# Everything behind the opening of a one-core attention and gated-MLP kernel as one written list of 1072 steps, with w_down of six token tiles by seven block products per pair

## The chip, the cores and the metric

The kernel runs on one core of one Trainium2 chip. The metric is the device time of an execution in microseconds (us), from launch to the last store; lower is better. The time before is the median of three runs.

## What is computed

A layer norm of 2048 tokens of width 512 feeds two branches in parallel, and both are added to the input:

```python
xn = layernorm(x)                                   # 2048 x 512
# A: linear attention, 32 heads of 16
q, k, v = split(xn @ wqkv)
phi_q = concat(softmax(q @ w_phi), softmax(-q @ w_phi))     # per head, 32 features
phi_k = the same of k
kv, z = phi_k^T v, sum of phi_k                     # per head, over the tokens
A = (phi_q kv / (phi_q z + 1e-6)) @ wo
# B: gated MLP without a nonlinearity
B = ((xn @ w_gate) * (xn @ w_up)) @ w_down          # 512 -> 1792 -> 512
out = x + A + B
```

Everything comes and goes in bf16.

## The kernel before

Tokens are worked in 16 tiles of 128; four tiles are a group of 512. x, all weights and the hidden values stay on the chip. Each engine runs its instructions in the order in which the program emits them (`manual_schedule`), so the order of the code is the order of the work, and a wait of one instruction holds all behind it on its engine.

- The opening (lines 550 to 602) loads, normalises and transposes the first four tiles, with v of these and half of two hidden units. TensorE's first instruction behind it is the second half of unit 0 (`unit(0, f, 2 * P, TT)`, line 627). All loads are issued at the top (lines 92 to 110) on SyncE's queue, in the order x, w_v, first columns of w_gate and w_up, the transposed w_k, then w_gate and w_up columns for units 2 to 3, 4 to 8 (around x tiles 4 to 7), 9 to 13, x from 8, w_down and w_o. The transposed load of w_q is issued at line 659, behind all transposes of x tiles 4 to 7.
- A unit (T, f) is 128 of the 1792 hidden columns for one group of 512 tokens: four matmuls for the gate, four for up, a copy of the gate out of PSUM (`gate_copy`, ScalarE), a multiplication on VectorE (`hidden`). Groups 0 and 1 are made so, 28 units.
- `fold` multiplies w_phi into the weights of k and q; `features` makes the softmax features: two exponentials on ScalarE, sums and reciprocals on VectorE, a multiplication on GpSimd. phi of q and the attention output `o_tok` are transposed by DMA (SyncE).
- Groups 2 and 3 of the gate and up products use Strassen's scheme in Winograd's form over pairs of blocks: `pair_block` has seven products p1 to p7, whose parts are kept (`keep`), joined (`join`) and multiplied. Its operands are differences of weights (`weight_sums`, line 445: GpSimd or VectorE, from bf16 to f16) and of tokens (`token_sums`); weights are scaled by powers of two first (`weight_norm`, line 420, `weight_scales`, `weight_up`).
- `fin_parts` (line 387) multiplies hidden values by w_down and attention output by w_o into one PSUM bank of 512 columns per tile: 14 + 4 matmuls. The store adds x on VectorE (line 398) and sends 128 KB. The last tile is cut into 384 and 128 columns.
- Order: hand-written loops with `ffn(1)` and `chore()` between projections, then `run_blocks` with fillers, then tiles 9 to 15 one after the other. Buffers rotate: of six PSUM banks of `ps_s` each new tile takes the next in turn.

Of the kernel before, what the change touches and what calls it, by code (L numbers as in the profile page):

```python
# [8 lines left out]
BF16 = mybir.dt.bfloat16  # L9
# [9 lines left out]
def _bcast_ap(ap_in: bass.AP, new_ap):  # L19
    return bass.AP(tensor=ap_in.tensor, offset=ap_in.offset, ap=new_ap)  # L20


@with_exitstack
def kernel(
# [40 lines left out]
    consts = ctx.enter_context(tc.tile_pool(name="consts", bufs=1))  # L65
    wpool = ctx.enter_context(tc.tile_pool(name="wpool", bufs=1))
# [7 lines left out]
    wgu = wpool.tile([P, 2, DC, F], BF16)  # L74
# [60 lines left out]
    xnT = xpool.tile([P, DC, HALF], BF16)  # L135
# [11 lines left out]
    for i in range(NV):  # L147
        vt = vpool.tile([P, 8, 4, E1], BF16, name=f"vt{i}", tag="vt")
        nc.vector.memset(vt[:, :, :, DH:E1], 1.0)
        vts.append(vt)  # L150
# [9 lines left out]
    def bank(name, dt=F32, n=TT):  # L160
        return ps_s.tile([P, n], dt, name=name, tag="s")
# [26 lines left out]
    def subtract(n, *means):  # L188
        xns[n] = xnpool.tile([P, D], BF16, name="xn", tag="x")
        nc.vector.tensor_scalar(out=xns[n][:], in0=xall[:, n, :], scalar1=means[0],  # L190
                                scalar2=means[1] if len(means) > 1 else None, op0=ALU.subtract,
                                **(dict(op1=ALU.subtract) if len(means) > 1 else {}))
# [9 lines left out]
    def centre_by_halves(n):  # L202
        h = D // 2
        part = consts.tile([P, 2], F32)
        junk = xnpool.tile([P, 2, h], BF16, name="junk", tag="x")
# [5 lines left out]

    chores = []

    def chore(k=1):
        for _ in range(min(k, len(chores))):
            chores.pop(0)()

    def ln_block(lo):
        mv = mv_tile()
        nb = lnpool.tile([P, GT], F32, name="nb", bufs=GT)  # L220
        rstd = []

        def scales():
            r = lnpool.tile([P, GT], F32, name="rstd", bufs=GT)
            ln_rstd(mv, GT, r[:])
            nm = lnpool.tile([P, GT], F32, name="nm")
            nc.gpsimd.tensor_scalar(out=nm[:], in0=mv[:, :, 0], scalar1=-1.0, scalar2=None, op0=ALU.mult)
            nc.gpsimd.tensor_tensor(out=nb[:], in0=nm[:], in1=r[:], op=ALU.mult)
            rstd.append(r)

        def apply(i):
            late = lo + i >= QT
            xn = xnpool.tile([P, D], F16 if late else BF16, name="xn", tag="x")
            if late:
                nc.gpsimd.tensor_scalar(out=xn[:], in0=xall[:, lo + i, :], scalar1=rstd[0][:, i:i + 1],
                                        scalar2=nb[:, i:i + 1], op0=ALU.mult, op1=ALU.add)
            else:
                nc.scalar.activation(out=xn[:], in_=xall[:, lo + i, :], func=AF.Identity,
                                     scale=rstd[0][:, i:i + 1], bias=nb[:, i:i + 1])
            nc.sync.dma_start(out=xt(lo + i), in_=xn[:], transpose=True)  # L240

        for i in range(GT):
            chores.append(lambda i=i: ln_stats(lo + i, mv[:, i, :]))
        chores.append(scales)
        for i in range(GT):
            chores.append(lambda i=i: apply(i))
# [18 lines left out]
    def fold(qk, dst, j0):  # L265
        R = P // 2
        banks = [bank("pq").rearrange("p (j c x) -> p j c x", j=2, c=DC) for r in range(2)]
        for j in range(2):
            for c in range(DC):
                for r in range(2):  # L270
                    rows = slice(r * R, (r + 1) * R)
                    nc.tensor.matmul(banks[r][:, j, c, :], lhsT=wT2[rows, qk, c, (j0 + j) * P:(j0 + j + 1) * P],  # L272
                                     rhs=bd[rows, c, 4 * r:4 * r + 4, :].rearrange("p a b -> p (a b)"),
                                     start=True, stop=True)
        dv = dst[:, j0:j0 + 2, :].rearrange("p j (c r x) -> p r j c x", c=DC, r=2)
        nc.scalar.copy(out=dv[:, 0], in_=banks[0])
        nc.vector.tensor_copy(out=dv[:, 1], in_=banks[1])

    def fold_both(qk, dst):
        for j0 in (0, 2):  # L280
            fold(qk, dst, j0)
# [6 lines left out]
    def features(n, w, name, pf=None):  # L288
        if pf is None:
            pf = bank(name)  # L290
            proj(pf, n, w)
        e = epool.tile([P, NG, 2, 4 * DH], F32, name="e")
        pfv = pf.rearrange("p (g c) -> p g c", g=NG)
        nc.scalar.activation(out=e[:, :, 0, :], in_=pfv, func=AF.Exp,  # L294
                             scale=rst[:, n:n + 1] if n < GT else 1.0)
        nc.scalar.activation(out=e[:, :, 1, :], in_=pfv, func=AF.Exp,  # L296
                             scale=nrst[:, n:n + 1] if n < GT else -1.0)
        ev = e[:].rearrange("p g s (h f) -> p (g s h) f", f=DH)
        sums = epool.tile([P, 2 * H], F32, name="sums")
        nc.vector.tensor_reduce(out=sums[:], in_=ev, axis=AX.X, op=ALU.add)  # L300
        rs = epool.tile([P, 2 * H, 1], F32, name="rs")
        nc.vector.reciprocal(out=rs[:].rearrange("p a b -> p (a b)"), in_=sums[:])  # L302
        phi = epool.tile([P, NG, P], BF16, name=f"phi{name}", tag="phi", bufs=4)
        nc.gpsimd.tensor_tensor(out=phi[:].rearrange("p g (x f) -> p (g x) f", f=DH), in0=ev,  # L304
                                in1=rs[:].to_broadcast((P, 2 * H, DH)), op=ALU.mult)
        return phi

    sends = []

    def qproj(n, held=False, new_bank=bank):  # L310
        q_begin(n, new_bank)
        q_end(held)

    q_open = []

    def q_begin(n, new_bank):
        pf = new_bank("q")
        proj(pf, n, W1q, lower)
        q_open.append((n, pf))

    def q_end(held=False):
        q_rest()
        q_features(held)

    def q_rest():
        n, pf = q_open[0]
        proj(pf, n, W1q, upper)

    def q_features(held=False):
        n, pf = q_open.pop()  # L330
        phiq = features(n, W1q, "q", pf)

        def send():
            phiqTs[n] = qtpool.tile([P, NG, P], BF16, name="phiqT")
            nc.sync.dma_start(out=phiqTs[n][:], in_=phiq[:].rearrange("p g c -> p (g c)"), transpose=True)

        sends.append(send)
        if not held:
            qsend()

    def qsend():
        sends.pop(0)()

    hTs = {}
    units = [(T, f) for T in range(NGRP // 2) for f in range(FC)]

# [7 lines left out]
    def gate_copy(ps, n):  # L354
        g_sb = gpool.tile([P, TT], BF16, name="g_sb")
        nc.scalar.copy(out=g_sb[:, 0:n], in_=ps)  # L356
        return g_sb

    def hidden(T, f, ps, g_sb, lo, hi):
        if T not in hTs:  # L360
            hTs[T] = hpool.tile([P, FC, TT], BF16, name="hT", tag="h")
        nc.vector.tensor_tensor(out=hTs[T][:, f, lo:hi], in0=ps, in1=g_sb[:, 0:hi - lo], op=ALU.mult)  # L362

    def unit(T, f, lo=0, hi=TT):
        pg = half(wg, "g", T, f, lo, hi)
        pu = half(wu, "u", T, f, lo, hi)
        hidden(T, f, pu, gate_copy(pg, hi - lo), lo, hi)

    def ffn(k):
        for _ in range(k):  # L370
            if units:
                unit(*units.pop(0))

    def fin_parts(n, new_bank, lo=0, hi=D):
        T, t4 = n // GT, n % GT
        w = hi - lo
        held = []

        rows = [(hTs[T][:, f, t4 * P:(t4 + 1) * P], wd[:, f, lo:lo + w]) for f in range(FC)]
        rows += [(oTs[n][:, c, :], wo[:, c, lo:lo + w]) for c in range(DC)]  # L380
        if n == 2 * GT:
            rows = [row for f, row in enumerate(rows) if f % FH != FH - 1 or f >= FC] + [rows[FH - 1], rows[FC - 1]]

        def mm(i):
            if i == 0:
                held.append(new_bank("fin")[:, 0:w])
            nc.tensor.matmul(held[0], lhsT=rows[i][0], rhs=rows[i][1], start=(i == 0), stop=(i == len(rows) - 1))  # L387
            if i == len(rows) - 1:
                store(held[0])

        def store(ps):
            o_sb = opool.tile([P, w], BF16, name=f"o_sb{w}", bufs=3 if w == D else 1)
            xres = xall[:, n, lo:lo + w]
# [9 lines left out]
    def fin(n, cuts=(0, D)):  # L403
        for lo, hi in zip(cuts, cuts[1:]):
            for part in fin_parts(n, bank, lo, hi):
                part()
# [427 lines left out]
```

## Time and profile before

| | |
|---|---|
| median of three runs | 216.29 us (216.26 to 216.33) |
| the profiled execution | 215.67 us |
| its span, first to last instruction | 213.9 us |
| TensorE busy (1280 matmuls) | 210.1 us |
| VectorE / ScalarE / GpSimd busy | 163.2 / 125.0 / 129.2 us |
| granted TensorE clock | 1.00 throughout |

The profile is of one execution. PE is TensorE, PEld its weight loads, DVE VectorE, ACT ScalarE, POOL GpSimd, SP SyncE, on whose queue all DMAs are issued. L387 is line 387 of the kernel. A matmul of the page has a modelled end, so its cost is read from the distance between starts, or from the chain.

### The profile page before, as it was taken

Reading aid. Unit: us, or ns where it says so; the run is one execution under the profiler, and the core shown is the slowest. Engines: PE = TensorE matmul, PEld = TensorE weight load, DVE = VectorE, ACT = ScalarE, POOL = GpSimd, SP = SyncE. Lnnn points to the kernel's source line nnn. Section 1 sums busy time; section 2 is a strip of 40 time slices with the busy share of each in tenths; the row PEclk is TensorE's granted clock in tenths of the full one; section 3 lists DMA queues with packets and bytes.
Section 4 is the critical chain, followed back from the end, with each engine's and each line's share of the span. In section 5 each row is a group of like instructions: output and inputs, shape, how many; then the busy total and the mean of one; then the engine's idle time right before and its main releaser. Section 6 shows DMA issues by size and latency. Waiting matters only on the chain.

```text
span 213.9 us, 3610 instructions
## 1 busy us (share of the span) xinstructions
PE 210.1 (98%) x1280; PEld 101.7 (48%) x1280; DVE 163.2 (76%) x279; ACT 125.0 (58%) x219; POOL 129.2 (60%) x112
## 2 busy tenths in 40 slices
PE   8999999999999999999999999999999999999994
PEld 3664445444444444554444444444444444444543
DVE  5757979869867788887777897988969689776341
ACT  4635578998896999442666686868746352220000
POOL 3600557597895788859899497979788620333000
PEclk9999999999999999999999999999999999999999
DMA  5999995613022023234444202021120201333511
GB/s 152 266 281 385 374 287 87 91 26 75 0 51 52 0 49 81 66 40 112 100 101 100 49 0 52 0 74 25 48 49 3 74 26 34 91 98 98 126 49 49
DMA packets 47249, 19.91 MB, mean 93 GB/s; under 512 B 37504, under 2 KB 46976, under 8 KB 47104
## 3 DMA queue, kind: packets, MB, share of 16 engines
q1 hardware_dynamic: 47232, 19.69, 36.6%
q8 instruction: 10, 0.16, 0.3%
q14 instruction: 7, 0.06, 0.1%
HBM read 8.67 MB, written 2.10 MB: 50 GB/s over the span
## 4 chain that ended last, share of the span: by engine, by line
PE 98%; ACT 1%; DVE 0%; issue 0%
PE fin L387 29%; PE g L350 11%; PE u L350 11%; PE sa L487 11%; PE pv L285 7%; PE q L285 6%; PE k L285 6%; PE sc L487 6%; PE sb L487 3%; PE kv L622 2%; PE ab L686 2%; PE warm L554 2%; PE pq L272 1%; PE tp L253 1%; ACT k L493 0%; ACT xnT L256 0%
## 5 line engine op out<-in xcount | busy, mean ns | idle before, releaser
L387 PE MATMUL fin<-wd,hT 128*128 128x512 bf16 (+2 forms) x238 | 54.1, 366 | 0.0
L304 POOL TENSOR_TENSOR phiq<-e,rs 128x1024 bf16<-128x1024 f32 x16 | 30.9, 1934 | 25.6 <-DVE rs L302 18.1
L304 POOL TENSOR_TENSOR phik<-e,rs 128x1024 bf16<-128x1024 f32 x16 | 30.9, 1933 | 24.2 <-DVE rs L302 17.3
L300 DVE TENSOR_REDUCE sums<-e 128x64 f32<-128x1024 f32 x32 | 38.7, 1208 | 9.0 <-ACT e L296 9.0
L350 PEld LDWEIGHTS <-wgu 128*128 128x128 bf16 x240 | 23.1, 98 | 24.2
L387 PEld LDWEIGHTS <-hT 128*128 128x128 bf16 x238 | 22.3, 98 | 24.4
L350 PE MATMUL u<-xnT,wgu 128*128 128x512 bf16 (+1 forms) x120 | 29.1, 365 | 0.0
L350 PE MATMUL g<-xnT,wgu 128*128 128x512 bf16 (+1 forms) x120 | 28.9, 365 | 0.0
L504 POOL TENSOR_TENSOR hT<-u_sb,hT 128x512 bf16<-128x512 bf16 x18 | 21.1, 1185 | 10.1 <-DVE u_sb L503 10.1
L362 DVE TENSOR_TENSOR hT<-u,g_sb 128x512 bf16<-128x512 f32 (+1 forms) x30 | 18.6, 622 | 4.5 <-PE u L350 3.9
L356 ACT CAST g_sb<-g 128x512 bf16<-128x512 f32 (+1 forms) x30 | 17.1, 569 | 8.1 <-PE g L350 7.9
L294 ACT ACTIVATE e<-q 128x512 f32<-128x512 f32 x12 | 7.2, 598 | 23.6 <-PE q L285 23.6
L302 DVE RECIPROCAL rs<-sums 128x64 f32<-128x64 f32 x32 | 17.7, 552 | 2.5
L493 ACT ACTIVATE k<-sa,both 128x512 f32<-128x512 f32 x21 | 14.5, 688 | 8.7 <-PE sa L487 8.6
L495 ACT COPY k<-sa 128x512 f32<-128x512 f32 x21 | 12.3, 587 | 11.2 <-DVE u_sb L503 7.4
L398 DVE TENSOR_TENSOR o_sb<-fin,xall 128x512 bf16<-128x512 f32 (+2 forms) x13 | 8.4, 646 | 12.0 <-PE fin L387 12.0
L445 POOL TENSOR_TENSOR T<-wgu,T 128x512 f16<-128x512 bf16 x14 | 17.0, 1216 | 0.5
L387 PE MATMUL fin<-wo,oT 128*128 128x512 bf16 (+2 forms) x68 | 17.1, 366 | 0.0
L487 PEld LDWEIGHTS <-T 128*128 128x128 f16 x112 | 10.8, 98 | 13.1 <-issue 0.6
L487 PE MATMUL sa<-ss,T 128*128 128x512 f16 x56 | 16.7, 379 | 0.1
L435 ACT ACTIVATE wgu<-wgu,up 128x1024 bf16<-128x1024 bf16 x14 | 15.9, 1156 | 0.1
L420 ACT ACTIVATE junk<-wgu 128x1024 bf16<-128x1024 bf16 x14 | 15.1, 1083 | 0.0
(98 smaller groups left out, 352.1 us busy)
## 6 DMA issues: line engine op xcount, KB each, us to landing
out_dram<-o_sb SPq DMA_DIRECT2D x15, 128.0 KB, 1.9
wd<-in_B_w_down_dram SPq DMA_DIRECT2D x1, 1792.0 KB, 15.4
wgu<-in_B_w_gate_dram SPq DMA_DIRECT2D x2, 640.0 KB, 6.8
wgu<-in_B_w_up_dram SPq DMA_DIRECT2D x2, 640.0 KB, 8.0
xall<-in_A_x_dram SPq DMA_DIRECT2D x1, 1024.0 KB, 12.1
xall<-in_A_x_dram SPq DMA_DIRECT2D x4, 128.0 KB, 2.7
vk<-in_A_wqkv_dram SPq DMA_DIRECT2D x2, 256.0 KB, 3.6
wgu<-in_B_w_gate_dram SPq DMA_DIRECT2D x2, 256.0 KB, 4.9
```

Of the source, the lines that this page charges most:

```text
L285: nc.tensor.matmul(ps, lhsT=xt(n)[:, j, :], rhs=w[:, j, :], start=(j == 0), stop=(j == DC - 1))
L300: nc.vector.tensor_reduce(out=sums[:], in_=ev, axis=AX.X, op=ALU.add)
L302: nc.vector.reciprocal(out=rs[:].rearrange("p a b -> p (a b)"), in_=sums[:])
L304: nc.gpsimd.tensor_tensor(out=phi[:].rearrange("p g (x f) -> p (g x) f", f=DH), in0=ev, in1=rs[:].to_broadcast((P, 2 * H, DH)), op=ALU.mult)
L350: nc.tensor.matmul(ps, lhsT=w[:, c, f * P:(f + 1) * P], rhs=xnT[:, c, T * TT + lo:T * TT + hi], start=(c == 0), stop=(c == DC - 1))
L356: nc.scalar.copy(out=g_sb[:, 0:n], in_=ps)
L362: nc.vector.tensor_tensor(out=hTs[T][:, f, lo:hi], in0=ps, in1=g_sb[:, 0:hi - lo], op=ALU.mult)
L387: nc.tensor.matmul(held[0], lhsT=rows[i][0], rhs=rows[i][1], start=(i == 0), stop=(i == len(rows) - 1))
L435: nc.scalar.activation(out=cols, in_=cols, func=AF.Identity, scale=up2[:, k, g:g + 1])
L445: (nc.gpsimd if i % 2 or k < 2 else nc.vector).tensor_tensor(out=t[:, i], in0=a, in1=b, op=ALU.subtract)
L487: nc.tensor.matmul(held[name], lhsT=w[:, j, :], rhs=x[:, j, :], start=start and j == 0, stop=(j == hc - 1), skip_group_check=True)
L504: (nc.vector if k == FH - 1 else nc.gpsimd).tensor_tensor(out=dst, in0=u[:], in1=dst, op=ALU.mult)
```

## The change

The loops behind the opening are replaced by steps with names. Each step is a function; one string, `ORDER`, lists all 1072 in the order of emission, with the engine behind a slash where a step may run on one of several (v VectorE, g GpSimd, a ScalarE). `SLOTS` gives for each buffer in turn the place that it takes, instead of rotation.

Names: g, u are a unit's products, gc its gate copy, h its multiplication; fk, fq folds with their copies fka, fkv, fqa, fqv; s, a, xt statistics, normalisation and transpose of a tile of x; k, vk, q projections, and x, y, r, i, p behind k or q the exponentials, sums, reciprocals and the multiplication to phi; qt and oT transposes; kv, ab products of attention, de, rd, ot its division; n, wr, wf, wp, ws the norms and scales of weights; up, t scaled weights and their differences; z token sums; p1 to p7, k1 to k3, j, m, d the block products with their copies, joins, multiplications and direct results; f, fs, fo the final products, sum and store of a tile (F: the last 128 columns of tile 12, which is now the one that is cut).

New is w_down of tiles 9, 10, 11 with 13, 14, 15: each pair (n, n + 4) takes seven block products over blocks of 896 hidden values by 256 columns (P1 to P7, each in parts a and b of four and three matmuls, w the four of w_o), where there were two times 14 matmuls of 512 columns. It needs scaled f16 copies of the quarters of w_down (cb, ct), their differences (wt, in two pieces each), sums of hidden values (S0 to S3 for each of seven blocks, written over weights already used), copies and additions (K, A, B) and joins of 256 columns (J); X stores a tile of 128 KB. Hidden values of groups 2 and 3 are f16 now. Weight scales come from sums of squares over a whole matrix instead of a bound per pair of blocks: 21 norms in place of 14, with w_down's.

The diff, cut:

```diff
+ORDER = """
+g0 u1 gc0/a wq n0.1 g1 gc1/v u0 h0 g3 h1 u3 gc3/a h3 fk0 fk2 fkv2/a s4 fkv0/v g7 g2 s5 g5 u2 gc2/a h2 =k fka0/a
+g12 gc7/a gc5/a u5 fka2/v gc12/a s6 u7 n1.6 k2 ky2 g6 k1 kx2 n0.2 g4 k3 h5 s7 s11 s10 s9 h7 s15 s8 gc6/a sc4 kx1
+kx3 ky1 ky3 gc4/a n0.6 g11 u4 u6 n2.1 a6/g a7/v s12 h4 h6 g9 u11 gc9/v kr2 a4/g a5/g xt6 xt7 u9 u12 h12 gc11/a
+n1.3 n0.3 n1.0 u10 g10 xt5 xt4 sc8 a8/g ki2 k0 kp2/g h11 gc10/a h9 h10 u8 g18 g8 u14 g14 kx0 kr1 s14 gc18/v n0.4
...
+k1.11/a p1.10 k1.10/a f7.0 f5.1 p3.9 f7.1 p2.11 p6.11 f5.6 f7.5 S0.3/v j2.12 m3.5/v p1.13 f7.2 j3.9 t52/v m3.9/v
+k2.11/a p7.11 k3.11/a j2.11 p2.13 p2.10 f7.6 p6.10 k1.13/v j2.13 t60/v f7.8 f7.7 f7.4 k2.10/a j2.10 p7.10
+k3.10/a fs5 qp10/g S1.3/v fs7 p5.11 cb22.1/a p5.10 =ab2 t61/g ab8 qt10 p6.13 j7.11 j7.10 t63/v de8/a p4.10 p6.12
+fo7 p4.11 p3.10 ct3.1/a t62/g rd8 d4.10/a q12.0 m2.11/g ot8 d4.11 m7.9/v j3.10 k2.12/a p7.12 ab10 k2.13/a p3.11
+q12.1 qp14/g de10/a m2.9/g k3.12/a rd10 ot10 fo1 qx12 qy12 p5.13 p7.13 q11.0 q11.1 p4.12 ab9 j3.11 qt13 k3.13/a
+j7.13 p5.12 m2.13/g S0.4/g S2.2/v p3.13 m7.11/v j7.12 d4.12/a qy11 P1b.10 f8.4 qx11 P1a.10 oT10 P1a.9 de9/a
+S0.5/v j3.13 rd9 qr15 qi15 S1.5/g S3.3/g m7.13/g P1b.9 f12.0 f12.5 p4.13 d4.13 ot9 K1.9/a P6a.9 cb21.1/a K1.10/a
+p3.12 S0.6/v j3.12 m3.11/v f8.3 S1.4/v cb22.0/a f8.1 S1.6/v m3.13/v ct3.0/a wt3.0/v P1a.11 ab13 P1b.11 cb21.0/a
+S2.5/g A1.9/g f8.2 oT8 f8.7 de13/a f12.6 qt14 oT9 f8.0 P6b.9 rd13 ot13 K6.9/a K1.11/a A6.9/g f8.5 f8.6 f8.8 oT13
+P6a.11 P5a.9 P5b.9 f12.3 P6b.11 S2.6/v qr11 qp15/g fs8 qr12 P6a.10 ab14 de14/a rd14 P6b.10 f12.2 f12.4 P7a.9
+P2b.9 fo5 P2w.9 P2a.9 K6.10/a qt15 ot14 wt3.1/g K5.9/a P7a.10 S2.4/g P7b.10 f12.1 qi12 oT14 wt4.1/v P7b.9
+K7.10/a qp12/g qt12 fo8 qi11 J2.9 P8w.9 P4b.10 P5a.10 P4w.10 ab15 wt4.0/v P4a.10 K7.9/v B6.9/g K6.11/v A7.10/g
+A7.9/g P5b.10 K5.10/a de15/v S3.5/v rd15 ot15 J8.9 P4w.9 P7a.11 P4a.9 P7b.11 K7.11/a S3.1/v oT15 J4.10 P4b.9
+P5a.11 ab12 P8w.10 de12/a qp11/g P4b.11 J4.9 P4a.11 J8.10 rd12 ot12 F12.1 F12.5 P2w.10 P4w.11 P5b.11 S3.2/g
+S3.4/g S3.6/g qt11 X13 oT12 K5.11/a J4.11 A7.11/g A6.10/g A1.11/g B6.10/g A1.10/g P3w.9 A6.11/g F12.0 ab11 P3b.9
+de11/v P3a.9 P2b.10 F12.2 J3.9 rd11 ot11 X9 X14 oT11 P8w.11 P3b.10 P3a.10 P3w.10 F12.3 J3.10 J8.11 B6.11/g F12.4
+P3b.11 P2a.10 J2.10 F12.6 f12.8 f12.7 fs12 fo12 P3a.11 F12.8 X10 X15 F12.7 P2a.11 P3w.11 Fs12 Fo12 J3.11 P2b.11
+P2w.11 J2.11 X11
+"""
+
+SLOTS = {
+    "s": (
+        "012345120345120345123405103125034102354013542301452015240354203254123051423014302143215243513025"
+        "13402340152430140323050310202045431204022354024114310254203453530130523140220532424"
+    ),
...
+}
...
+    def ring(pool, tag, shape, dt, name):
+        return pool.tile(shape, dt, name=name, tag=f"{tag}{next(slots[tag])}", bufs=1)
...
     def bank(name, dt=F32, n=TT):
-        return ps_s.tile([P, n], dt, name=name, tag="s")
+        return ring(ps_s, "s", [P, n], dt, name)
...
+    def copy(eng, dst, src, scale=None):
+        if eng is A and scale is None:
+            A.copy(out=dst, in_=src)
+        elif eng is A:
+            A.activation(out=dst, in_=src, func=AF.Identity, scale=scale)
+        elif scale is None:
+            eng.tensor_copy(out=dst, in_=src)
+        else:
+            eng.tensor_scalar(out=dst, in0=src, scalar1=scale, scalar2=None, op0=ALU.mult)
...
-        for f in range(2):
-            unit(0, f, 2 * P, TT)
-        del units[0:2]
-        ffn(1)
-        fold_both(1, W1k)
-        ffn(1)
...
-        for n in range(GT, NT):
-            vkproj(n)
-            chore()
-            ffn(1)
-            if n in (9, 10):
-                fold(0, W1q, 2 * n - 18)
-            kv(n - 2)
-            chore(2 if n == 4 else 1)
-            if n >= 12:
-                qproj(n - 12)
-            norm(2 if n < 6 else 1)
...
+    def unit_steps(u):
+        T, f = u // FC, u % FC
+        lo = 2 * P if u < 2 else 0
+
+        @step(f"g{u}")
+        def _():
+            held["g", u] = half(wg, "g", T, f, lo, TT)
+
+        @step(f"gc{u}", A)
+        def _(eng):
+            held["gc", u] = gate_copy(held.pop(("g", u)), TT - lo, eng)
+
+        @step(f"u{u}")
+        def _():
+            held["u", u] = half(wu, "u", T, f, lo, TT)
+
+        @step(f"h{u}")
+        def _():
+            hidden(T, f, held.pop(("u", u)), held.pop(("gc", u)), lo, TT)
+
...
+    @step("wq")
+    def _():
+        nc.sync.dma_start(out=wT2[:, 0, :, :], in_=A_wqkv[:, 0:D], transpose=True)
...
+    def weight_norm(k, g):
+        junk = ring(xnpool, "x", [P, 1024], BF16, "junk")
+        cols = pair_cols(k)[:, g] if g < 2 else wd[:, 2 * k:2 * k + 2, :]
+        out = junk[:].rearrange("p (c h f) -> p c h f", c=DC, h=2) if g < 2 else junk[:].rearrange("p (c f) -> p c f", c=2)
+        with nc.allow_low_precision(reason="a bound for a power of two"):
+            A.activation(out=out, in_=cols, func=AF.Square, accum_out=nrm[:, g, k:k + 1])
...
+    W = D // 2
+    quarters = {11: wd[:, 0:FH, 0:W], 12: wd[:, 0:FH, W:D], 21: wd[:, FH:FC, 0:W], 22: wd[:, FH:FC, W:D]}
+    PIECES = ((0, 4), (4, FH))
+    dT = {}
...
+    def down_copy(name, quarter):
+        def run(eng, lo, hi):
+            copy(eng, down_tile(name)[:, lo:hi], quarters[quarter][:, lo:hi], up3[:, 2:3])
+
+        for i, (lo, hi) in enumerate(PIECES):
+            steps[f"c{name}.{i}"] = (lambda eng, lo=lo, hi=hi: run(eng, lo, hi), A)
+
+    def down_sub(name, a, b):
+        def run(eng, lo, hi):
+            eng.tensor_tensor(out=down_tile(name)[:, lo:hi], in0=down_tile(a)[:, lo:hi], in1=down_tile(b)[:, lo:hi],
+                              op=ALU.subtract)
+
+        for i, (lo, hi) in enumerate(PIECES):
+            steps[f"w{name}.{i}"] = (lambda eng, lo=lo, hi=hi: run(eng, lo, hi), V)
+
+    for name, quarter in (("b11", 11), ("t1", 12), ("t2", 22), ("t3", 12), ("b21", 21), ("b22", 22)):
+        down_copy(name, quarter)
+    down_sub("t1", "t1", "b11")
+    down_sub("t2", "t2", "t1")
+    down_sub("t3", "b22", "t3")
+    down_sub("t4", "b21", "t2")
+
+    wgu16 = wgu[:].bitcast(F16)
+
+    def hidden_sum(i, k, eng):
+        tok = slice(t0 * P, TT)
+        S = [wgu16[:, j // 2, t0:GT, ((j % 2) * FH + k) * P:((j % 2) * FH + k + 1) * P] for j in range(4)]
+        A11, A12, A21, A22 = (hT(T)[:, k + h * FH, tok].rearrange("p (t x) -> p t x", x=P) for T in (2, 3) for h in (0, 1))
+        a, b, op = ((A21, A22, ALU.add), (S[0], A11, ALU.subtract), (A11, A21, ALU.subtract), (A12, S[1], ALU.subtract))[i]
+        eng.tensor_tensor(out=S[i], in0=a, in1=b, op=op)
+
+    for k in range(FH):
+        for i in range(4):
+            steps[f"S{i}.{k}"] = (lambda eng, i=i, k=k: hidden_sum(i, k, eng), G)
+
+    def pair_steps(n):
...
+        def mms(ps, rows, first):
+            if first and ps not in mine:
+                mine[ps] = bank("d" + ps)
+                mine[ps, "new"] = True
+            for l, r in rows:
+                nc.tensor.matmul(mine[ps][:, 0:W], lhsT=l, rhs=r, start=bool(mine.pop((ps, "new"), False)),
+                                 stop=True, skip_group_check=True)
+
+        def product(p, ps, l, r, first=False, attn=None):
+            for name, ks in (("a", range(0, 4)), ("b", range(4, FH))):
+                steps[f"P{p}{name}.{n}"] = (lambda ks=ks: mms(ps, [(l(k), r(k)) for k in ks], first), None)
+            if attn:
+                attention(f"P{p}w", ps, *attn, first)
+
+        def attention(name, ps, t, c, first=False):
+            steps[f"{name}.{n}"] = (lambda: mms(ps, [(oTs[t][:, j, :], wo[:, j, c * W:(c + 1) * W]) for j in range(DC)],
+                                                first), None)
+
+        def kept(name):
+            tile_name, j = dict(k1=("ka", 0), k5=("ka", 1), k2=("kb", 0), k3=("kb", 1))[name]
+            if tile_name not in mine:
+                mine[tile_name] = ring(xnpool, "x", [P, 2, W], F32, "dK")
+            return mine[tile_name][:, j, :]
+
+        def keep(name, p, ps):
+            steps[f"K{p}.{n}"] = (lambda eng: copy(eng, kept(name), mine[ps][:, 0:W], inv), A)
+
+        def add(name, p, other):
+            steps[f"{p}.{n}"] = (lambda eng: eng.tensor_tensor(out=kept(name), in0=kept(name), in1=other(), op=ALU.add), G)
+
+        def join(p, t, c, ps, other):
+            def run():
+                if ("o", t) not in mine:
+                    mine["o", t] = ring(opool, "o", [P, D], BF16, "o_sb")
+                V.scalar_tensor_tensor(out=mine["o", t][:, c * W:(c + 1) * W], in0=mine[ps][:, 0:W], scalar=inv,
+                                       in1=other(), op0=ALU.mult, op1=ALU.add)
+
+            steps[f"J{p}.{n}"] = (run, None)
+
+        product(1, "a", a(2, 0), d("b11"), True)
+        keep("k1", 1, "a")
+        add("k1", "A1", lambda: x(n, 0))
+        product(2, "b", a(2, FH), B21, True, (n, 0))
+        join(2, n, 0, "b", lambda: kept("k1"))
+        product(5, "d", s(0), d("t1"), True)
+        keep("k5", 5, "d")
+        product(6, "a", s(1), d("t2"))
+        keep("k2", 6, "a")
+        add("k2", "A6", lambda: x(n, 1))
+        add("k2", "B6", lambda: kept("k5"))
+        product(3, "c", s(3), d("b22"), True, (n, 1))
+        join(3, n, 1, "c", lambda: kept("k2"))
+        product(7, "a", s(2), d("t3"))
+        keep("k3", 7, "a")
+        add("k3", "A7", lambda: x(m, 1))
+        attention("P8w", "d", m, 1)
+        join(8, m, 1, "d", lambda: kept("k3"))
+        product(4, "a", a(3, FH), d("t4"), False, (m, 0))
+        join(4, m, 0, "a", lambda: x(m, 0))
+        for t in (n, m):
+            steps[f"X{t}"] = (lambda t=t: nc.sync.dma_start(out=out_view(t, t + 1)[:, 0, :], in_=mine["o", t][:]), None)
+
+    t0 = 1
+    LAST = 12
+    QF = (8, 9, 13, 10, 14)
+    paired = tuple(T * GT + i for T in (2, 3) for i in range(t0, GT))
...
+    for word in ORDER.split():
+        name, _, eng = word.partition("/")
+        fn, default = steps.pop(name)
+        if default is None:
+            fn()
+        else:
+            fn(engines[eng] if eng else default)
+    assert not steps, sorted(steps)
+    stack.pop().close()
```

The list's first rows, and all from S0.3 to the end, are shown; the opening's own code and the loads' are as before.

## The prediction

> **What bounds the kernel now.** I read the page first: busy shares and the chain that ended last.
>
> ```profile
> PE 210.1 (98%) x1280; PEld 101.7 (48%) x1280; DVE 163.2 (76%) x279; ACT 125.0 (58%) x219; POOL 129.2 (60%) x112
> PE 98%; ACT 1%; DVE 0%; issue 0%
> ```
>
> TensorE is busy for 98% of the span, and 98% of the chain is TensorE. So its own work is the time: a matmul taken away shortens the kernel, and every wait put in front of one lengthens it. The chain in order of time gives the price of a matmul:
>
> ```profile
> 8.86 0.87 PE g L350 x8
> 11.89 0.44 PE g L350 x4
> ...
> 13.64 0.86 PE g L350 x4
> ...
> 15.36 0.57 PE pq L272 x32
> ...
> 91.47 3.88 PE fin L387 x18
> ```
>
> Eighteen of 512 columns take 3.88 us, 0.2157 each; eight of 256 columns take 0.87, 0.109 each, so half width costs half. By windows, TensorE is busy for 199.17 of the 199.30 us from 11.9 to 211.2 and VectorE for 155.73 (78%). The opening, which the change leaves, ends at 11.89; there the list begins.
>
> The loads that land late are read next, tile by tile, the last part of x that the first steps touch and two chunks of w_gate:
>
> ```profile
> L83 SPq DMA_DIRECT2D xall<-in_A_x_dram x1: 504/504/504, 12.2 to 12.2; - x1
> DMA to landing us min/median/max: 7.8/7.8/7.8
> ```
>
> ```profile
> L86 SPq DMA_DIRECT2D wgu<-in_B_w_gate_dram x1: 577/577/577, 11.0 to 11.0; - x1
> DMA to landing us min/median/max: 4.6/4.6/4.6
> ```
>
> ```profile
> L86 SPq DMA_DIRECT2D wgu<-in_B_w_gate_dram x1: 633/633/633, 12.7 to 12.7; - x1
> DMA to landing us min/median/max: 9.1/9.1/9.1
> ```
>
> So x tiles 4 to 7 are there at 12.2 + 7.8 = 20.0, w_gate's columns of units 4 to 8 at 15.6, of units 9 to 13 at 21.8. The kernel before uses each of these later than that and hides them.
>
> Last, VectorE beside GpSimd, in the timelines of both at one weight difference (line 445):
>
> ```profile
> 122.85 1.71 DVE L445 TENSOR_TENSOR T<-wgu 128x512 f16<-128x512 bf16 x2
> ```
>
> ```profile
> 123.01 1.27 POOL L504 TENSOR_TENSOR hT<-u_sb,hT 128x512 bf16<-128x512 bf16 x1 [1.42 <-DVE u_sb L503]
> 124.24 1.33 POOL L445 TENSOR_TENSOR T<-wgu,T 128x512 f16<-128x512 bf16 x1
> ```
>
> ```profile
> L445 DVE TENSOR_TENSOR T<-wgu x10: 414/894/1378, 122.8 to 161.2; 128x512 f16<-128x512 bf16 x10
> ```
>
> The same instruction takes 414 ns alone and 1378 when GpSimd is in a multiplication: the second of the pair ends at 124.56, one run's length after GpSimd's first ends. The mean wait is 894 - 414 = 480 ns.
>
> **The change, part by part.** *w_down of six tiles.* Away go 6 x 18 matmuls of 512 columns: 108 x 0.2157 = 23.30. Each of three pairs brings 7 products x 7 blocks and 4 x 4 for w_o, 65 of 256 columns: 195 x 0.109 = 21.26. All lie on the path: **-2.04**. The second weight-scale matmul has 7 columns and costs nothing (the 14-column one took 169 ns, modelled, beside others).
>
> *The one wait inside the blocks.* At 114.7 TensorE stands for 0.25 us for a copy of ScalarE; the list puts other matmuls there. **-0.25**, or nothing.
>
> *The first ten microseconds of the list.* TensorE's order is g0 u1 g1 u0 (16 x 0.109 = 1.74, to 13.63), g3 u3 (1.73, to 15.36), the folds fk0 fk2 (0.57, to 15.93), g7 g2 g5 u2 g12. Four steps from other queues stand in front:
> ScalarE has gc0, then n0.1, then gc3. n0.1 squares columns of units 1 and 8 and so waits for 15.6; at 1.083 + 0.224 it ends at 16.9, gc3 (0.60) at 17.5. By the list of places, g7 takes the PSUM bank of g3: it begins at 17.5, not 15.93, and g5 ends at 20.1.
> VectorE has h3, then s4, then fkv0. s4 takes statistics of x tile 4 and waits for 20.0; it ends (0.67 + 0.18) at 20.8, the copy fkv0 (0.68) at 21.5. u2 takes the bank that fkv0 empties: it begins at 21.5, where without waits it would begin at 18.52.
> g12 then meets its columns, there since 21.8. TensorE has lost **+2.94**. Had the first two waits gone, g12 alone would hold it from 19.39 to 21.8, +2.4. Nothing hides this: from here on TensorE has no spare time. Bounds: 0, if the loads land three microseconds earlier, and 3.5, if they land half a microsecond later; I take what the rows give. Later first uses (units 9 to 13 of w_up, x from 8, w_down's norms) come after their loads once this wait is paid.
>
> *Steps moved on SP.* The transposing load of w_q goes ahead of all others, behind w_o's issue (16.44 + 8.24 = 24.7, where it stood at 35.3); its 2.72 us on SP pass no transfer that is due, since the first transpose of the list (xt6) waits for x from 4 and the first use of w_q is folded some 50 us later. Transposes of phi and o take 2.7 and 2.3 us to land; the tightest is tile 11's phi, due to land some 2.5 us before its matmuls if GpSimd keeps time. Nothing, then.
>
> *VectorE's load.* Behind the opening it had 155.7. Added: nine gate copies and six block copies out of PSUM (15 x 0.68, the row of line 277: 10.2), three more copies of v (2.0) less two of the folds (-1.4), six more multiplications (0.424: 2.5), six w_down differences and eleven hidden sums in f16 (an estimate from that row by length, 0.75 and 0.35: 8.4), four weight scalings, a normalised tile and one copy of w_down between SBUF places (0.65 to 0.35, estimated from the 354 ns of line 190: 3.5), two copies and twelve half-wide joins for six stores (2.2), less eight denominators gone to ScalarE (-1.5). Together about 26, so 182 beside TensorE's 196.6: 93%. ScalarE and GpSimd stay at 70 to 75%. VectorE has become nearly as long as TensorE, and in order.
>
> *The waits between VectorE and GpSimd.* The kernel before has 13 VectorE instructions of the kinds that read two SBUF tensors, or one at doubled speed, behind its opening; the list has 42, and 22 of them in its last 44.5 us of TensorE work, where VectorE's rows sum to 44.2, less the overlap of neighbours (163.2 busy against 170.5 of the rows) 42.3. Queued behind each are the joins that empty PSUM banks, and for those TensorE waits. Bounds: no wait at all, as five of the ten T's had, gives 0; the T's mean, 22 x 0.48 = 10.6, less the 2.2 us that VectorE has free and some 1 that the banks hold in reserve, gives +7.4. I take 0.2 us for each, since many of these sums come where GpSimd itself waits for VectorE, as in the rows above: 4.4 - 3.3 = **+1.1**.
> The Trainium skill (SBUF — State Buffer, SBUF: two separate sides) has this as an exclusive lock held for the whole instruction, for VectorE instructions with two SBUF inputs against a GpSimd instruction that reads SBUF. The trace agrees: 964 ns of extra time in the row above. Taken for every such step with GpSimd at 75%, it speaks for the upper bound, and against this change.
>
> *The end.* The last join is of 256 columns (0.42 by line 362's half-wide row, 0.45 with a scalar) where it was 0.29, and the last store 128 KB where it was 32 KB (1.9 against 1.5 us by the medians, 1.7 against 1.5 among the last three): **+0.35**.
>
> Sum: -2.04 - 0.25 + 2.94 + 1.1 + 0.35 = +2.1. The profiled execution has 213.9 of span and 215.67 in all, 1.8 around it; after: 217.8. The median of the runs shown, 216.29, lies 0.62 above the profiled one, so 218.4.
>
> **The rivals.** *The saving arrives.* If the opening loads are no wait (they would have to land about three microseconds earlier, or the copies not stand behind them) and the lock costs half a microsecond, the sum is -2.04 - 0.25 + 0.35 + 0.5 = -1.4: 214.9; with no wait at all 214.3. For it: the saving itself is exact, and TensorE's other rows stay. Against it: the three landing times above, which nothing in the change moves. It decides from under 1.5 us of new waits in all. 0.27.
> *Early wait only, saving eaten.* 2.94 and no lock: +1.0, 217.3; with the early wait at 2.4 and no loss at the end, +0.1, 216.4. The second is the narrow case of no measurable difference (0.08, taken within 0.2% or 0.43 us, which is about what a measurement of this kernel can tell); the first belongs to the forecast.
> *VectorE becomes the bound in the last quarter.* The lock is paid in full: +7.4 in place of +1.1, 224.7; with half of it, 221.5. For it: 42.3 of 44.5 us are taken before any wait. Against it: five of ten T's met an idle GpSimd. 0.17.
> *The products do not shorten TensorE*, if 256-column matmuls were held by their weight loads: those take 98 ns each in PEld against 109, so it holds here; no chance of its own.
>
> **How the numbers follow.** Forecast, early wait and a little lock: 0.48, 218.4, own range 216.8 to 220. The lock in full 0.17, all slower; no difference 0.08; faster 0.27. Slower: 0.48 + 0.17 = 0.65. The range leaves out the best tenth of the faster case and the worst part of the lock: 214.3 to 223.0.
>
> **What would show it.** Right: a TensorE gap of about 1.5 us near 16 to 17.5 ended by ScalarE's g copy, and one of about 1.4 near 20 to 21.5 ended by a VectorE copy of a fold, itself behind statistics that wait for x; TensorE's matmuls 1280 - 108 + 195 + 1 = 1368; VectorE busy over 180 us; S, w and m steps on VectorE in two kinds, near their lone time and a microsecond longer; TensorE's later gaps at bank places whose last reader is a VectorE join. Wrong: TensorE at 99% from 12 us on with no early gap (the saving arrives), or early gaps of this size and a time under 216 (then some other part is shorter than its rows), or waits for transposes of phi or o, which I cost at nothing.

## The result, and the profile after

The changed kernel takes 219.7 us (median of 4 runs, 219.4 to 219.9) where the kernel before took 216.3 beside it: ratio 1.0157, interval 1.014 to 1.0175, slower by 3.4 us. The profiled execution has 219.66 us and a span of 217.9. Forecast: 218.4, with 217.8 for the profiled execution.

Busy shares of the page after (TensorE's weight loads give the number of matmuls, 1368 as forecast; 20 matmul records are missing):

```profile
PE 207.8 (95%) x1348; PEld 109.9 (50%) x1368; DVE 188.3 (86%) x327; ACT 132.4 (61%) x239; POOL 156.9 (72%) x147
```

TensorE has less to do and takes longer. The view of TensorE's waits says for what (in all, times, longest). It has one more row, `warm`, from the opening, which is the only one that the kernel before has:

```profile
PE g L331 <- ACT g_sb L337: 1.6, 1, 1.6
PE u L331 <- DVE vk L341: 1.3, 1, 1.3
PE g L331 <- DVE hT L351: 0.9, 1, 0.9
PE ab L609 <- DVE otok L637: 0.8, 1, 0.8
PE ab L609 <- DMA phiqT<-phiq: 0.2, 1, 0.2
```

Five waits, each met once. The timeline gives the first two, at the places forecast (17.5 and 21.5):

```profile
15.95 1.06 ACT L696 ACTIVATE junk<-wgu 128x1024 bf16<-128x1024 bf16 x1 [3.12 <-DMA wgu<-in_B_w_gate_dram]
17.01 0.57 ACT L337 CAST g_sb<-g 128x512 bf16<-128x512 f32 x1
17.62 2.75 PE L331 MATMUL g<-xnT,wgu 128*128 128x512 bf16 x11 [1.59 <-ACT g_sb L337]
20.16 0.69 DVE L255 BATCH_NORM_STATS2 stats<-xall 128x6 f32<-128x512 bf16 x1 [1.86 <-DMA xall<-in_A_x_dram]
20.99 0.66 DVE L341 CAST vk<-pq 128x512 bf16<-128x512 f32 x1
21.70 1.02 PE L331 MATMUL u<-xnT,wgu 128*128 128x512 bf16 x4 [1.32 <-DVE vk L341]
```

Read each chain from its bracket: ScalarE stands 3.12 us for w_gate's columns, then makes the norm n0.1 and only then the copy that g7 needs; VectorE stands 1.86 us for x, makes s4's statistics and only then the fold copy that u2 needs.

Further on in the timeline, around 65 to 70 us, is the third wait:

```profile
65.10 3.83 POOL L541 TENSOR_TENSOR phik<-e,rs 128x1024 bf16<-128x1024 f32 x2
67.10 1.85 DVE L724 TENSOR_SCALAR up<-up 128x2 f32<-128x2 f32 x1
69.07 0.67 DVE L351 TENSOR_TENSOR hT<-u,g_sb 128x512 bf16<-128x512 f32 x1
69.79 1.02 PE L331 MATMUL g<-xnT,wgu 128*128 128x512 bf16 x4 [0.89 <-DVE hT L351]
```

An instruction over two numbers per partition (the step ws0) takes 1.85 us: it ends with GpSimd's phi (65.10 + 3.83 = 68.93). Queued behind it is a product hT that empties a bank, and TensorE waits for that bank. Around 175 us:

```profile
175.39 1.94 POOL L541 TENSOR_TENSOR phiq<-e,rs 128x1024 bf16<-128x1024 f32 x1
175.50 2.11 DVE L756 TENSOR_TENSOR T<-wgu,T 128x512 f16<-128x512 bf16 x1
177.96 0.69 DVE L637 TENSOR_TENSOR otok<-ab,rden 128x512 bf16<-128x512 f32 x1
178.70 0.41 PE L609 MATMUL ab<-KV,phiqT 128*128 128x68 bf16 x8 [0.78 <-DVE otok L637]
```

The weight difference t63, 0.41 us when alone, takes 2.11 behind a phi; otok comes late, and the next attention with it.

I measure a gap as the time from one matmul's start to the next beyond the first one's own columns. Counting gaps of 0.25 us and more behind 12 us, there are 1.75 + 1.49, then 1.05, 0.32 and 0.94, in all 5.55 us, against one of 0.25 before. TensorE's last matmul ends at 214.73 (before 211.16).

### The profile page after: what moved, and what is told of

Read it like the earlier page. It is cut to its first block, busy times and chain, and to the rows that moved or that the text cites. A ratio compares the mean times of both kernels' runs of the same rounds, so it can differ in the third digit from the quotient of the medians.

```text
span 217.9 us, 3839 instructions
## 1 busy us (share of the span) xinstructions
PE 207.8 (95%) x1348; PEld 109.9 (50%) x1368; DVE 188.3 (86%) x327; ACT 132.4 (61%) x239; POOL 156.9 (72%) x147
## 5 line engine op out<-in xcount | busy, mean ns | idle before, releaser
L531 DVE TENSOR_REDUCE sums<-e 128x64 f32<-128x1024 f32 x32 | 38.5, 1203 | 1.1 <-ACT e L519 1.0
L661 PE MATMUL fin<-wd,hT 128*128 128x512 bf16 (+2 forms) x148 | 37.4, 359 | 0.3
L661 PEld LDWEIGHTS <-hT 128*128 128x128 bf16 (+1 forms) x154 | 14.6, 98 | 13.6
L519 ACT ACTIVATE e<-q 128x512 f32<-128x512 f32 x24 | 13.3, 601 | 11.3 <-PE q L317 11.1
L536 DVE RECIPROCAL rs<-sums 128x64 f32<-128x64 f32 x32 | 17.5, 546 | 1.4
L337 ACT CAST g_sb<-g 128x512 bf16<-128x512 f32 (+1 forms) x21 | 11.5, 555 | 8.9 <-PE g L331 8.8
L260 POOL TENSOR_SCALAR ve<-mv 128x1 f32<-128x1 f32 (+1 forms) x7 | 2.1, 294 | 19.4 <-DVE mv L256 19.3
L519 ACT ACTIVATE e<-k 128x512 f32<-128x512 f32 x24 | 13.8, 603 | 3.2 <-PE k L317 2.1
L339 ACT ACTIVATE k<-sa 128x512 f32<-128x512 f32 x18 | 10.7, 596 | 7.2 <-PE sa L795 7.1
L317 PEld LDWEIGHTS <-x 128*128 128x128 f16 x96 | 9.2, 98 | 10.9
L817 POOL TENSOR_TENSOR hT<-u_sb,hT 128x512 f16<-128x512 bf16 x12 | 14.3, 1207 | 0.1
L317 PEld LDWEIGHTS <-xnT 128*128 128x128 bf16 x96 | 8.9, 98 | 10.5 <-ACT xnT L305 1.3
```

Of the source, the lines that this page charges most:

```text
L317: nc.tensor.matmul(ps, lhsT=xt(n)[:, j, :], rhs=w[:, j, :], start=(j == 0), stop=(j == DC - 1))
L337: A.copy(out=dst, in_=src)
L519: A.activation(out=held[s + "e", n][:, :, sign, :], in_=held[s, n].rearrange("p (g c) -> p g c", g=NG), func=AF.Exp, scale=(nrst if sign e ...
L531: V.tensor_reduce(out=sums[:], in_=ev(), axis=AX.X, op=ALU.add)
L536: V.reciprocal(out=rs[:].rearrange("p a b -> p (a b)"), in_=held.pop((s + "s", n))[:])
L661: nc.tensor.matmul(held["fin", n, lo], lhsT=l, rhs=r, start=len(done) == 1, stop=len(done) == FC + DC)
```

## The experiments

The order's rows are those of the list. The first four ran beside a kernel before of 215.7 us, the next four beside 215.5 on the same chip.

**The first two waits, each step behind the copy it held up** (e1_queues):

```
-gc0/a wq n0.1 g1 gc1/v u0 h0 g3 h1 u3 gc3/a h3 fk0 fk2 fkv2/a s4 fkv0/v g7
+gc0/a wq g1 gc1/v u0 h0 g3 h1 u3 gc3/a n0.1 h3 fk0 fk2 fkv2/a fkv0/v s4 g7
```

> Two steps are moved in the list, each only on its own engine: the first weight norm (n0.1) behind the gate copy gc3 on ScalarE, and the copy fkv0 ahead of the statistics s4 on VectorE. The load of w_gate's columns of units 9 to 13, which g12 needs, still lands near 21.8 us. Theory (queued copies behind late loads are only half the story, the load of g12 waits underneath): g7 and u2 no longer wait, g12 waits instead about 2.4 us for the load; the time falls by 0.5 us, to about 219.2. Rival 1 (the two queued copies are the whole early loss): it falls by 2.9, to 216.8. Rival 2 (VectorE is the bound, early gaps of TensorE cost nothing): unchanged at 219.7.

Measured 220.1, ratio 1.0205 (1.018 to 1.0229): nothing won. Both early gaps are gone and one of 2.56 us stands at 21.5, where g12 waits for columns that landed at 21.44: the wait underneath that the prediction had at +2.4 is real. The timeline's row, and the window behind it, whose granted clock is the third number from the end:

```profile
21.49 1.66 PE L331 MATMUL g<-xnT,wgu 128*128 128x512 bf16 x4 [2.39 <-DMA wgu<-in_B_w_gate_dram]
21.80:25.10 3.30, 3.30 (x10) 1.10 (x9) 1.69 (x5) 1.63 (x3) 0.00 (x0) 0.50 1.02 377
```

Behind that gap the trace grants half the clock for 3.41 us, from 21.76 on, and eight matmuls start 0.43 us apart where 0.22 is usual: some 1.7 us more. Three of the six executions have the mean clock of this one, 0.992, and the three at the full clock took 219.2 to 220.0 us: the expected gain of 0.5 does not show in those either.

**An order of the opening steps that waits for no load** (e2_early):

```
-g0 u1 gc0/a wq n0.1 g1 ... fkv2/a s4 fkv0/v g7 g2 s5 g5 u2 ... g12 gc7/a ...
+g0 u1 gc0/a wq g1 ... gc3/a n0.1 h3 fk0 fk2 fkv2/a fkv0/v g7 g2 g5 u2 gc2/a h2 s4 s5 ...
+g6 gc7/a gc5/a u5 fka2/v gc6/a s6 u7 k2 ky2 g12 ...
```

> The early part of the list is put in an order that meets no load that is still under way: the two moves of the run before, g12 exchanged with g6 (and their copies), statistics of later tiles of x spread behind the multiplications that are due earlier, two weight norms moved back on ScalarE. No instruction is added or taken away. Theory (TensorE has no spare time, so the early gap is paid in full): the gap of 2.9 us between 12 and 25 us goes, and the time falls by 2.5 to 2.9, to 216.8 to 217.2; the waits near 69, 104 and 178 us stay. Rival (VectorE, 86% busy, is the bound from there on): VectorE's work comes due earlier and TensorE waits later for what it won; the time falls by less than 1, to 218.7 or more.

Measured 220.0, ratio 1.0216 (1.018 to 1.0252): nothing won. TensorE has no gap until 34 us, and then two that the changed kernel has not, 0.71 at 34.7 and 2.02 at 38.5. The timeline of this run there:

```profile
38.48 1.69 PE L331 MATMUL g<-xnT,wgu 128*128 128x512 bf16 x7 [1.85 <-DMA xnT<-xn]
```

The product g18 waits there, and the releaser named is the transposes of x, which stand on SP behind w_q's transposing load (24.03 to 31.85). That gave the theory of e5 and e6 below. It holds for this gap, as e6 shows, but not for the time.

**The first weight scale of w_up in single columns** (e3_ws):

```
-            V.tensor_scalar(out=u.bitcast(I32), in0=u.bitcast(I32), ...)
-            V.tensor_scalar(out=u, in0=u, scalar1=levels[lo], ...)
+            for c in range(lo, hi):
+                w = up3[:, c:c + 1]
+                ...
```

> Only the two VectorE instructions on the 128x2 weight scales (ws0) are changed: each is made as two instructions on one column, 128x1. In the changed kernel the 128x2 multiplication took 1854 ns, to the end of GpSimd's phi, and the 128x1 one of w_down's scale 155 ns while GpSimd was in a difference. Theory (the two-column form takes the port that GpSimd holds, the one-column form doesn't): the four instructions take about 0.15 us each, VectorE reaches the multiplication behind them 2 us earlier, TensorE's gap of 1.05 us at 69.8 goes and the time falls by 0.8 to 1.1, to 218.6 to 218.9. Rival (any small instruction waits there, or the gap has another cause): the last instruction still ends with GpSimd's, and the time stays at 219.7.

Measured 218.3, ratio 1.0126 (1.0107 to 1.0146), and the gap at 69.8 is gone. Its timeline beside the same phi:

```profile
65.78 3.82 POOL L541 TENSOR_TENSOR phik<-e,rs 128x1024 bf16<-128x1024 f32 x2
67.12 0.15 DVE L726 TENSOR_SCALAR up<-up 128x1 f32<-128x1 f32 x1
67.37 0.15 DVE L726 TENSOR_SCALAR up<-up 128x1 f32<-128x1 f32 x1
```

Two instructions of one number per partition take 0.15 us each in the middle of a phi that held up one of two numbers for 1.85.

**The step t63 behind the otok that TensorE waits for** (e4_t63):

```
-... j7.10 t63/v de8/a ... m2.11/g ot8 d4.11
+... j7.10 de8/a ... m2.11/g ot8 t63/v d4.11
```

> Only one VectorE step is moved: the weight difference t63, which took 2106 ns near 175.5 us because GpSimd was in a multiplication of phi, goes behind the division of tile 8's attention (ot8), for which TensorE's next attention product waits. Theory (lock on the queue): the division comes about 2 us earlier, TensorE's gap of 0.94 us at 178.7 goes, and the time falls by 0.6 to 0.9, to 218.8 to 219.1; t63 waits at its new place too, if GpSimd is busy then. Rival (VectorE is late there anyway): another VectorE step is late in its place, no change above 0.2 us.

Measured 218.2, ratio 1.0115 (1.0098 to 1.0132); the gap at 178.7 is gone; t63 takes 1.04 us at its new place. Beside the changed kernel's ratios of 1.0157 and 1.0166 (e0_after), e3 is worth 0.7 to 0.9 us and e4 0.9 to 1.1. So each of the late waits is worth about its length (1.05 and 0.94), and their cause is a VectorE step that stands behind a GpSimd phi and ahead of the step that empties a bank.

**The changed kernel itself, and w_q's load behind the transposes, alone and with the early order** (e0_after, e5_wq, e6_early_wq), to find what ate the early 3 us. e5's edit, made on e2's order in e6:

```
-gc0/a wq n0.1 g1 ...           -... u10 g10 xt5 xt4 sc8 ...
+gc0/a n0.1 g1 ...              +... u10 g10 xt5 xt4 wq sc8 ...
```

> The changed kernel as it is, as the base for the three others. 219.7 (219.4 to 220.1), with two early gaps on TensorE of 1.6 to 1.9 us and 1.3 to 1.6 us, and the later ones of 1.05 us at 69.8, 0.3 us at 104 and 0.95 us at 179. Both theories: the same.

> One part alone: the step that issues w_q's transposing load goes on SP behind the transposes of x for tiles 4 to 7, instead of ahead of all of them. Theory (the moved load delays those transposes by its some 8 us on SP, but the two early gaps come first and cover it): no gain, 219.7 within 0.3, and the gaps are those of the changed kernel. Rival (w_q's move costs time by itself): 219.2 or less.

> Both together: the early order that waits for no load (as run before, which gave no time back) and w_q's load behind the transposes of tiles 4 to 7. Theory (the early gaps of 3.2 us went to 34 to 39 us, because the transposes sit on SP behind w_q, and ScalarE's weight norms wait for the buffers that those transposes release): TensorE has no gap over 0.3 us before 60 us, and the time is 219.7 - 3.2 + 0.3 = 216.8 (216.4 to 217.5). Rival 1 (the wait at 38 us is in the order of ScalarE's work itself, not in SP's queue): the gap of 2 us stays, 219.0 to 220. Rival 2 (VectorE is the bound from 120 us on, so time won early is lost there): no early gap, but new ones behind 120 us that add up to 2 us or more, 219 to 220.

Measured 219.4 (1.0166, 1.0143 to 1.0188), 219.4 (1.0166, 1.014 to 1.0191) and 219.6 (1.0186, 1.0164 to 1.0207). Moving w_q changes nothing in the time, alone or with the early order. In e6 the transposes begin 4 us earlier, and gaps of 0.71 at 34.9 and 1.92 at 42.2 stand. The second is not that of e2:

```profile
36.82 1.89 PE L331 MATMUL g<-xnT,wgu 128*128 128x512 bf16 x8
42.19 1.02 PE L331 MATMUL u<-xnT,wgu 128*128 128x512 bf16 x4 [1.75 <-ACT e L519]
```

g18 starts at 36.82 and waits no more (38.48 in e2). But u18 starts at 42.19, where in e2 it started at 42.03, with no gap of its own. So a second wait, for ScalarE's exponential, stood under the first, and ends at the same time: as in e1, taking away the upper one wins nothing. The theory of SP's queue was right for one gap and wrong as the whole. The next kernel's timeline shows the second chain.

**All four edits** (c2_all: early order, w_q behind, ws0 in columns, t63 moved):

> The four edits together: early order, w_q behind the transposes, the first weight scale of w_up in single columns, and the step t63 behind ot8. Theory (five named waits make up the whole loss): 216.8 - 1.05 - 0.94 = 214.8 (214.4 to 215.6), below the kernel before at 216.3. Rival (time won early meets the lock waits on VectorE later): 216 or more, with new gaps on TensorE behind 60 us.

Measured 217.2, ratio 1.0079 (1.0054 to 1.0104), 2.4 over the theory, and the rival's place is wrong too: behind 60 us only 0.28 is left. What is left is 0.71 at 34.7 and 1.91 at 42.0. The timeline there:

```profile
34.93 0.23 POOL L260 TENSOR_SCALAR ve<-mv 128x4 f32<-128x4 f32 x1 [3.18 <-DVE mv L256]
35.55 0.52 DVE L536 RECIPROCAL rs<-sums 128x64 f32<-128x64 f32 x1
36.98 0.77 POOL L500 TENSOR_SCALAR xn<-xall,rstd,nb 128x512 f16<-128x512 bf16 x1
37.71 1.93 POOL L541 TENSOR_TENSOR phik<-e,rs 128x1024 bf16<-128x1024 f32 x1
39.68 0.69 ACT L519 ACTIVATE e<-k,rst 128x512 f32<-128x512 f32 x1 [1.39 <-POOL phik L541]
41.30 0.68 ACT L519 ACTIVATE e<-k,nrst 128x512 f32<-128x512 f32 x1
42.03 1.02 PE L331 MATMUL u<-xnT,wgu 128*128 128x512 bf16 x4 [1.75 <-ACT e L519]
```

From the bottom: u18 needs the bank that k0's second exponential empties; the first of the two waits for an exponential buffer; tile 2's phi frees that; and the phi stands on GpSimd behind sc8 and a8 (ve to xn), which waited 3.18 us for statistics on VectorE. The list has "sc8 a8/g ki2 k0 kp2/g": a phi that is due now behind scalars that are due at 47 us. In the changed kernel TensorE came 3 us later here, and its trace has no gap over 0.25 us between 22 and 69 us.

**The order mended along that chain** (f1_all, on c2):

```
-... gc9/v s15 kr2 a4/g a5/g xt6 xt7 u9 u12 h12 s8 s12 gc11/a
+... gc9/v a4/g a5/g xt6 xt7 s8 u12 h12 kr2 ki2 kp2/g u9 gc11/a
-... xt5 xt4 wq sc8 a8/g ki2 k0 kp2/g h11 gc10/a h9 h10 u8 ... gc18/v n0.4 ky0 kr0 ...
+... xt5 xt4 wq k0 h9 h11 s12 gc10/a s15 sc8 a8/g h10 u8 ... gc18/v ky0 n0.4 kr0 ...
-... p2.0 qy4 ab3 f2.2 ...
+... p2.0 qy4 f2.2 ab3 ...
```

> The four edits of the run before (217.2, with TensorE gaps of 0.71 us at 34.7, 1.91 at 42.0 and 0.28 at 102.4 left), and the order mended at those three places: the phi of tile 2 on GpSimd goes ahead of the layernorm scalars and the normalised x of tile 8, with its reciprocal on VectorE ahead of the statistics of tiles 12 and 15; w_up column u12 and its product h12 go ahead of u9; one weight norm goes behind an exponential on ScalarE; one block of w_down goes ahead of the attention of tile 3. Theory (the gap at 42 us is a chain: u18's bank waits for ScalarE's exponential, that for the buffer that GpSimd's phi frees, and the phi stands in GpSimd's queue behind scalars that wait for VectorE's statistics): no gap over 0.4 us behind 12 us, last matmul at 209 to 209.5, 217.2 - 0.71 - 1.91 - 0.28 = 214.3 (213.9 to 215.2), which is below the kernel before. Rival (VectorE's lock waits behind 120 us take back what is won): new gaps on TensorE behind 120 us of 1.5 us or more in all, 216 or more.

Measured 215.40 against 215.83 beside it, ratio 0.998 (0.9968 to 0.9993): below the kernel before, by 0.2%. The phi now begins at 34.59 and no gap of 1.9 us is left. The same queue, in this run's timeline:

```profile
34.59 1.93 POOL L541 TENSOR_TENSOR phik<-e,rs 128x1024 bf16<-128x1024 f32 x1 [2.95 <-DVE rs L536]
37.65 0.68 ACT L519 ACTIVATE e<-k,rst 128x512 f32<-128x512 f32 x1
41.04 1.02 PE L331 MATMUL g<-xnT,wgu 128*128 128x512 bf16 x4 [0.49 <-DVE g_sb L341]
```

ScalarE's exponential no longer waits. The time is 1.1 over the theory, for gaps of 0.31 at 35.1, 0.66 at 41.0 (the last row) and 0.30 at 103.5, where up50 on VectorE (1.91 us behind GpSimd) now holds the otok that the next attention waits for. Behind 120 us there is none of 0.25 us or more, so the rival's loss there did not come.

**Those three mended** (g1_all, on f1):

```
-... kr2 ki2 kp2/g u9 gc11/a ... wq k0 h9 h11 ... kx0 kr1 s14 gc18/v ... up50/v
+... kr2 u9 h9 ki2 kp2/g gc11/a ... wq k0 h11 ... kx0 gc18/v kr1 s14 ... up50/a
```

> The run before (215.4) with the three waits mended that its trace still names: the product h9 goes ahead of a reciprocal on VectorE (0.31 us of TensorE at 35.1), the copy gc18 ahead of a sum and a statistic on VectorE (0.66 at 41.0), and the scaling up50 goes from VectorE to ScalarE (0.30 at 103.5: up50 took 1.91 us behind GpSimd, and the attention of tile 3 stands behind it). Theory (each named gap of TensorE is worth its length): no gap over 0.3 us behind 12 us, 215.4 - 1.27 = 214.1 (213.8 to 214.9). Rival (as each gap goes, the next queue shows another of its size): 215.0 or more, with new gaps of 0.7 us or more in all.

Measured 215.29 against 215.78, ratio 0.9974 (0.9959 to 0.9988). The three gaps are gone, and 0.35 at 38.0, 0.32 at 43.5 and 0.24 at 47.2 stand in their place: the rival. Its waits view has two rows in the place of the five above, 0.2 us each: a product u for ScalarE's copy g_sb, and a product g for VectorE's hT.

## Why the prediction was right, and where its sizes were off

The case that I forecast came: slower, for an early wait for loads and some lock waits between VectorE and GpSimd. Term by term, in the profiled executions:

| step | forecast | measured |
|---|---|---|
| w_down by products | -2.04 | -2.0 |
| the wait at 114.7 | -0.25 | -0.25 |
| early wait | +2.94 | +3.24 |
| steps moved on SP, transposes | 0 | +0.32 |
| VectorE behind GpSimd | +1.1 | +1.99 |
| the end | +0.35 | +0.45 |
| gaps of 0.08 to 0.25 us, not forecast | 0 | +0.3 |
| sum (spans 213.9 and 217.9) | +2.1 | +4.0 |

- *w_down.* Last matmul less all gaps from 0.08 us on (those the length of one missing record left out): 210.33 before, 208.32 after. The same kernel in e0_after, whose trace lacks no record, gives 208.38. 256-column matmuls cost half, as priced.
- *Early wait.* Both places, both queues and both releasers are as forecast; the loads landed at 15.79 and 20.14, 0.2 us later than before, and the gaps are 0.3 us longer. e1 shows the third wait underneath. What the working lacked was the next one: it asked what is late if two waits go and found g12's load, and neither the transposes that g18 meets then (e2) nor the chain to u18 under them (e6, c2).
- *SP.* e5 bears out w_q's load at nothing in this order, though by cover: it held SP's queue for 7.71 us where I had 2.72, ahead of the transposes of x, and the early waits hid that. Transposes of phi were not quite nothing: 0.32 at 104, where the landing of phiqT is the last to come; f1, with a block of w_down ahead of that attention, waits there for otok instead (0.30).
- *VectorE behind GpSimd* is the term that was mis-sized, and its sum was not the right one. I priced 22 steps in the last 44.5 us at 0.2 us each, 4.4, less some slack. The trace has 18 such steps from 170.2 to 214.7. Over the shortest time of their kind they waited 4.7 us in all, 1.7 of it t63 alone and eleven of them under 0.06. TensorE paid 0.94, for t63, and has no other gap of 0.25 us there. So the +1.1 fits that stretch, but by one long wait and not by the sum: partly luck. What the term left out is 1.05 for ws0 at 67, outside the stretch and of a kind for which I had priced no wait. TensorE waited for an hT and an otok, not for the joins that I named. e3 and e4 took these two away one at a time.
- *VectorE's load* was forecast at 182 us behind the opening and measured at 188.3 - 7.2 = 181.1. That these agree is luck: the measured time holds some 14 us of waits behind GpSimd (for the steps that read two SBUF tensors or scale one, each one's time over the shortest of its kind), and the forecast's only the 4.8 of the kernel before. So the work grew by some 16 us, and not by 26. Two windows, one where VectorE is fullest and one of the last 44.5 us of TensorE's work (TensorE busy in the third column, VectorE in the fifth):

```profile
180.00:195.00 15.00, 14.87 (x114) 9.56 (x114) 14.78 (x29) 9.30 (x17) 8.61 (x9) 1.00 0.37 62
170.20:214.70 44.50, 43.54 (x368) 30.95 (x368) 39.16 (x72) 18.74 (x35) 33.27 (x32) 1.00 0.40 85
```

Where VectorE is fullest, 14.78 of 15, TensorE stands for 0.13 us: VectorE is not the bound there. In the last 44.5 us it is busy for 39.2, waits included, where the working had 42.3 without any. (The rows of before that it used for the overlap sum to 173.4, not 170.5, which makes 41.6 of the 42.3.) So the rival of the lock in full did not even have its condition in the stretch that it named. The waits themselves are there, as a group of the changed kernel shows (shortest, median and longest ns of the six):

```profile
L756 DVE TENSOR_TENSOR T<-wgu x6: 407/416/1622, 74.3 to 171.4; 128x512 f16<-128x512 bf16 x6
```

Four of the six ran at their lone time, one paid 0.33 us and one 1.2: a wait is rare and long, not some 0.2 us for each.

The median came out 1.3 us over the forecast, and the profiled execution 1.9: the 0.62 that I added for the median of before has no counterpart after, whose profiled execution (219.66) is at its median. That the median is closer to its forecast than the sum, +2.1 against +4.0, is luck too.

So the saving did not arrive because the new order's waits are over twice as long as it. With those waits mended it does in part: g1 stands 0.5 us below the kernel before, where 2.0 and the 0.25 at 114.7 are saved, and 0.45 is lost at the end, 0.9 in gaps from 0.24 us on and some 0.3 in shorter ones. The loss against the kernel before is thus due to the order and the form of ws0, not to the products, which g1 keeps; that products with the order of before would win the whole 2 us was not tried.

## What to carry to other kernels

When an engine runs at 98%, every step of another in-order engine that stands ahead of the one that empties its bank must be asked what it waits for: a load, a buffer, another engine. Mending one such wait can show the next, which the first had covered (e1, e6), so follow the queue past the mended place before counting the gain. A wait between two engines is worth what the bound engine pays for it, at the few places where its cover is thin, and not its own sum.

## What the runs showed of the hardware that was not expected

A scaling of 128x2 f32 on VectorE stood 1.85 us behind GpSimd's phi, and one of 128x1 took 0.15 us beside it; one of 128x1024 bf16 took 0.48 us alone and 1.90 beside one. The Trainium skill (SBUF — State Buffer, Who interferes with whom) says that such an operation can enter a mode that takes the ports shared with GpSimd. The traces agree in the 1.85 us for two numbers per partition; the 0.15 us for one shows no such wait.

The same loads land at different times in different executions: x tiles 4 to 7 between 18.48 (e2, issued at 11.74) and 20.89 us (e3, issued at 12.76), with the same loads ahead of them. A wait for a load differs with that: e4, with x at 18.81, lost 1.12 and 0.67 us where e3 lost 1.84 and 1.78.

The releaser that a view names is the last to come for that one instruction, and tells nothing of what stands behind it: at 38.5 in e2 it named the transposes, rightly, and with those out of the way (e6) the time won was lost again at 42.2, behind a phi.
